# Later places for V and for keys by tokens in a delta-rule kernel's order of transfers

## The chip, the core and the metric

The kernel runs on one core of one Trainium2 chip. The metric is the time of one execution on the device in microseconds; five executions of the kernel before gave a median of 535.37 us (534.04 to 536.3).

Engines are named as in the profile: PE is the matrix engine and PEld its weight loads, DVE the vector engine, ACT the scalar engine, POOL the general engine, SP the engine whose queue issues most of the loads. Each engine runs its own queue strictly in order; between queues there are semaphores.

## The reference

Two blocks follow each other. The first is a delta-rule attention over 768 tokens for 4 batches, 8 heads and a head size of 48, everything in float32:

```
k_n = k / (norm(k) + 1e-6)
for t in range(768):
    y[t]  = q[t] @ state
    v_old = state.T @ k_n[t]
    state = state + beta[t] * outer(k_n[t], v[t] - v_old)
```

The second takes the result as 3072 rows of 384 numbers, sends each row to one of 8 experts by a hash of its token id, and computes `relu(x @ w1[e]) @ w2[e]` (384 to 1024 to 384) with that expert's weights.

## The kernel before, in words

**Chunks and groups.** The 768 tokens are cut into 24 chunks of 32 tokens (`C = 32`, `NU = 24`). Four chunks make a group (`GC = 4`), so there are six groups, numbered from 0. The four batches lie in the four quarters of the 128 partitions. Inside a chunk the recurrence over tokens is replaced by a triangular system, so that the state only has to be carried from chunk to chunk.

**Work for a group.** `load_turn(g, a, b)` (line 359) loads the keys (`a = 0`, tile `Kt`) or queries (`a = 1`, tile `Qt`) of 128 tokens for one batch: eight loads of 192 KB for a group. `turn(g, a, b)` (line 381) transposes such a tile on PE (L389) and copies it on ACT into `KQ` (L394). There is one `Kt` and one `Qt` buffer for each batch, so a group's tile can only be loaded when the same tile of the group before has been transposed. `gram(c)` (line 400) then multiplies keys with keys and queries for a chunk on PE (L415); ACT copies the first product into `GK` (L425), and DVE multiplies the second with a triangular mask into `GQ` (L431). Group 0 has its own form for the keys (L447). `inverse(g)` (line 494) takes the four `GK` of a group, transposes them (`NT`, L506), normalizes, writes the diagonal of U on ACT (L530), and inverts the triangular matrices by 31 elimination steps on DVE, each a multiply (L546) and an add (L544). `turn_back(g)` transposes U into `TU` (L560).

**Work for a chunk.** `spread_t` makes `Tz` from `TU` on ACT (L472), `scale_v(c)` multiplies `V` with the keys' norms on DVE into `V1` (L491; two buffers), and `chunk(c)` (line 594) is the recurrence: PE forms the state's answer to the keys (L581, with V1 added by L613), ACT copies it to R (L618), PE solves (L632), ACT copies W (L646), PE updates the state (L653) with the keys by tokens `K4`, ACT copies the new state (L676), and PE forms the chunk's output (L689), which ACT copies (L698) and POOL scatters into a scratch array in the order of the experts (L703). Chunk 0 has no state yet and solves straight from V1.

**The loads by chunk.** `load_k(c)` (line 365) loads the keys by tokens into one of three `K4` buffers, four loads of 48 KB, one for each batch. `load_v(c)` (line 372) does the same for V with four buffers. All `Kt`, `Qt`, `K4` and `V` loads of the attention block go through SP's queue.

**The order.** No engine's order is written by hand. `task(...)` (line 190) only notes a piece of work: its engine, an estimated duration, what it reads and writes, and some hints. `order()` (line 223) is a list scheduler that runs when the kernel is built. It walks through a model of all engines, and each time takes, on the engine that can start first, the ready task with the longest estimated chain of work behind it (`rest`). A transfer of n KB occupies the model's single transfer channel for `n * 6.3` ns (line 333). The argument `hold` is the earliest time in the model at which a task that waits for nothing else counts as ready (lines 249 and 352). It isn't a wait on the chip: it only moves the task in the order that results. The instructions are then emitted in the order of the planned start times, with the semaphores that the data need. Mask multiplies carry `boost=1e6` and so go ahead of everything else that is ready on DVE. Where the plan leaves PE idle for more than 380 ns, up to a planned time of 80,000 ns, `fill` puts some matmuls into a free bank (L986).

**After the chunks** come the eight experts (lines 1003 to 1163): rows are gathered (L1017), transposed (L1036), multiplied with both weight arrays (L1044, L1078, L1060) and scattered to the output (L1067).

Of the kernel before, what the change touches and what calls it, by code (L numbers as in the profile page):

```python
# [20 lines left out]
def kernel(  # L21
# [88 lines left out]
    with ExitStack() as phase1:  # L110
# [19 lines left out]
        def quarter(b):  # L130
            return slice(C * b, C * b + C)
# [58 lines left out]
        def task(eng, ns, reads, writes, emit, words=0, kb=0, more=0, boost=0, job=None,  # L190
                 hold=0, claim=(), slack=0):
            deps = {writer[r] for r in reads if r in writer}
            for w in writes:
                deps |= readers.get(w, set())
                if w in writer:
                    deps.add(writer[w])
            i = len(tasks)
            deps.discard(i)
            tasks.append(dict(eng=eng, ns=ns, deps=deps, emit=emit, words=words, kb=kb,
                              more=more, boost=boost, job=job, hold=hold,  # L200
                              claim=claim, slack=slack))
            for r in reads:
                readers.setdefault(r, set()).add(i)
            for w in writes:
                writer[w] = i
                readers[w] = set()
            return i
# [157 lines left out]
        def load_k(c):  # L365
            dst = K4s[c % 3].rearrange("p u r d -> p (u r) d")
            for b in range(B):
                task("SP", 500, (), (f"k4{c % 3}{b}",), lambda b=b: nc.sync.dma_start(
                    out=dst[quarter(b), :, 0:D], in_=k_r[b][c * C:(c + 1) * C]), kb=48,
                    hold=16000)  # L370

        def load_v(c):
            for b in range(B):
                task("SP", 500, (), (f"v{c % 4}{b}",), lambda b=b: nc.sync.dma_start(
                    out=Vs[c % 4][quarter(b)], in_=v_r[b][c * C:(c + 1) * C]), kb=48,
                    hold=16000)

        def four(name):
            return tuple(f"{name}{b}" for b in range(B))
# [496 lines left out]
        def note():  # L876
# [29 lines left out]
            for g in range(1, GC):  # L906
                for b in range(B):
                    for a in range(2):
                        load_turn(g, a, b)
                if g == 1:  # L910
                    for c in range(2):
                        load_k(c)
                        load_v(c)
                    load_v(2)
                    load_v(3)
                for b in range(B):
                    for a in range(2):
                        turn(g, a, b)
                if g < GC - 1:
                    for c in range(GC * g, GC * g + GC):  # L920
                        gram(c)
                    inverse(g)
                    if g == 1:
                        turn_back(1)
# [4 lines left out]
            for c in range(NU):  # L929
                g, cc = divmod(c, GC)  # L930
                if c + 2 < NU:
                    load_k(c + 2)
                if c + 4 < NU:
                    load_v(c + 4)
                if c + 1 < NU:
                    spread_t(c + 1)
                    masks_of(c + 1)
                chunk(c)
                if c + 2 < NU:
                    scale_v(c + 2)  # L940
                if cc == GC - 1 and 2 <= g + 2 < NG:
                    turn_back(g + 2)
                if g + 4 < NG and cc == GC - 1:
                    for b in range(B):
                        for a in range(2):
                            load_turn(g + 4, a, b)
                            turn(g + 4, a, b)
                n = c + 3 * GC
                if n < NU:
                    gram(n)  # L950
                if n < NU and n % GC == GC - 1:
                    inverse(n // GC)
# [239 lines left out]
```

## Time and profile before

| what | value |
|---|---|
| median of five executions | 535.37 us |
| the profiled execution's own time | 536.39 us |
| its span on the core | 534.6 us |
| first chunk's solve begins (L632) | 67.62 us |
| last row store issued (L703) | 238.5 us |
| PE busy, share of the span | 481.8 us, 90% |
| DVE busy | 246.4 us, 46% |
| ACT busy | 186.3 us, 35% |
| POOL busy | 96.6 us, 18% |
| mean granted clock of PE | 0.954 |

The profile is of one execution. A line of a timeline gives the start and the duration in us, the engine, the line of the kernel, the operation, what it writes and reads, and in brackets how long the engine stood idle before it and on whose account. In a table by stretches each engine's busy time stands with the number of its instructions in brackets, and the last three columns are the clock granted to PE (1 is full speed), the mean busy share of the transfer engines, and GB/s. In the slices each digit is the busy share of 13.4 us, in tenths.

The SP queue issues, in this order: the keys and queries of group 0 (0.9 to 9.0 us), the keys and queries of group 1 (9.1 to 19.4), 20 loads of V and K4 for the first chunks (19.4 to 33.2), group 2 (33.2 to 43.2), 16 more loads of K4 and V (43.2 to 53.3), group 3 (53.3 to 61.9) and group 4 (61.9 to 71.5). From then on loads of V and K4 alternate as the chunks free their buffers.

The time at which the state-carrying copy W (L646) of a chunk begins shows the pace of the chunks: chunk 0 at 69.3 us, 4 at 99.1, 8 at 129.6, 12 at 160.4, 16 at 190.0, 20 at 221.3.

### The profile page before, as it was taken

What the parts mean: (1) busy time and instruction counts of PE and PEld (TensorE: products, weight loads), DVE (VectorE), ACT (ScalarE), POOL (GpSimd) and SP (SyncE); (2) the same over time, 40 slices, a digit from 0 to 9 for tenths busy, and PEclk for the clock granted to TensorE, in tenths of its full rate; (3) what the DMA queues carried; (4) which work ended last, traced back from release to release, by engine and by line L of the source; (5) the groups of instructions that cost most, each with busy time, mean ns of one, the idle gap of its engine ahead of it and who ended that gap; (6) DMA issues with size and microseconds to landing.
All of it is one profiled execution on the core that took longest, in us unless ns stands there. A gap on an engine that the chain in (4) does not pass through costs nothing. (4 is left out here: it accounts for less than half of the span.)

```text
span 534.6 us, 15771 instructions
## 1 busy us (share of the span) xinstructions
PE 481.8 (90%) x6700; PEld 322.0 (60%) x6700; DVE 246.4 (46%) x775; ACT 186.3 (35%) x406; POOL 96.6 (18%) x139
## 2 busy tenths in 40 slices
PE   8868699899999898865999999999999999999990
PEld 6646577677777677653565555555655556555650
DVE  9688779998999998523120111201202111111100
ACT  4623497988798785320101001101011010100100
POOL 6000011111111112226113111302303111102010
PEclk9968699999999999995999999999999999999996
DMA  9767983574343344713704417107134171340000
GB/s 143 136 108 113 163 143 85 120 156 98 84 86 78 77 99 147 205 48 110 273 14 175 150 34 255 60 13 273 55 119 167 39 258 37 109 155 28 14 28 15
DMA packets 119127, 59.75 MB, mean 112 GB/s; under 512 B 104202, under 2 KB 112614, under 8 KB 119056
## 3 DMA queue, kind: packets, MB, share of 16 engines
q1 hardware_dynamic: 103664, 22.04, 23.1%
q10 hardware_dynamic: 10272, 22.14, 11.6%
q0 software_dynamic: 5120, 14.56, 8.1%
q8 instruction: 53, 0.87, 0.7%
q14 instruction: 18, 0.15, 0.1%
HBM read 49.90 MB, written 10.42 MB: 113 GB/s over the span
## 5 line engine op out<-in xcount | busy, mean ns | idle before, releaser
L1044 PE MATMUL h_ps<-xT,w_sb 128*128 128x378 f32 (+3 forms) x384 | 132.1, 498 | 4.0 <-DVE h_sb L1049 3.3
L1044 PEld LDWEIGHTS h_ps<-xT,w_sb 128*128 128x128 f32 x384 | 72.7, 193 | 56.4 <-issue 17.4
L1049 DVE TENSOR_SCALAR h_sb<-h_ps 128x378 f32<-128x378 f32 (+3 forms) x32 | 18.0, 563 | 152.2 <-PE h_ps L1044 152.2
L1078 PE MATMUL oT_ps<-h_sb,w_sb 128*128 128x424 f32 (+1 forms) x192 | 68.0, 507 | 0.0
L546 DVE TENSOR_TENSOR tmp<-U,Ni 128x60 f32<-128x60 f32 (+15 forms) x186 | 62.0, 338 | 4.5 <-ACT U L530 1.1
L1060 PE MATMUL o_ps<-w_sb,h_sb 128*126 128x384 f32 (+1 forms) x192 | 63.6, 486 | 0.0
L544 DVE TENSOR_TENSOR U<-U,tmp 128x60 f32<-128x60 f32 (+15 forms) x186 | 62.0, 339 | 3.3
L1067 POOL DMA_INDIRECT out_dram<-o_sb,idx_i x28 | 27.7, 988 | 194.7 <-ACT o_sb L1066 144.2
L703 POOL DMA_INDIRECT x_scratch<-x_sb,slot x24 | 24.7, 1030 | 193.8 <-ACT MT L472 69.6
L1078 PEld LDWEIGHTS oT_ps<-h_sb,w_sb 128*128 128x128 f32 x192 | 35.5, 190 | 25.6 <-issue 13.9
L1047 ACT ACTIVATE h_sb<-h_ps 128x378 f32<-128x378 f32 (+3 forms) x32 | 15.9, 496 | 99.2 <-PE h_ps L1044 83.3
L1060 PEld LDWEIGHTS o_ps<-w_sb,h_sb 128*126 128x126 f32 (+1 forms) x192 | 35.0, 186 | 23.7
L676 ACT ACTIVATE S<-psS 48x384 f32<-48x384 f32 (+1 forms) x92 | 42.8, 465 | 13.6 <-PE psS L653 8.7
L1066 ACT COPY o_sb<-o_ps 126x384 f32<-126x384 f32 (+3 forms) x16 | 7.7, 479 | 83.5 <-PE o_ps L1060 69.0
L1017 POOL DMA_INDIRECT xg<-x_scratch,rows_i x28 | 28.3, 1010 | 34.3 <-DVE idx_i L1028 18.1
L653 PE MATMUL psS<-W,K 32*128 32x96 f32 x736 | 26.8, 280 | 5.1 <-ACT W L646 4.9
L1080 ACT COPY oT<-oT_ps 128x424 f32<-128x424 f32 (+1 forms) x8 | 4.0, 499 | 75.3 <-PE oT_ps L1078 75.3
L1038 DVE COPY xT<-xT_ps 128x318 f32<-128x318 f32 (+3 forms) x28 | 14.0, 499 | 33.8 <-PE xT_ps L1036 33.8
L689 PEld LDWEIGHTS psY<-W,MT 64*64 64x64 f32 x704 | 22.7, 134 | 10.0 <-issue 9.1
L653 PEld LDWEIGHTS psS<-W,K 32*128 32x128 f32 x736 | 23.0, 186 | 8.3 <-ACT W L646 6.7
L689 PE MATMUL psY<-W,MT 64*64 64x48 f32 x704 | 25.9, 220 | 0.2 <-issue 0.2
L472 ACT ACTIVATE Tz<-TU,kmask 128x256 f32<-128x256 f32 x40 | 24.9, 727 | 1.0 <-DVE TU L560 0.9
(162 smaller groups left out, 604.0 us busy)
## 6 DMA issues: line engine op xcount, KB each, us to landing
w_sb<-in_moe_w_dram ACTq DMA_DIRECT2D x14, 1536.0 KB
Kt<-in_k_dram SPq DMA_DIRECT2D x24, 192.0 KB
Qt<-in_q_dram SPq DMA_DIRECT2D x24, 192.0 KB
V<-in_v_dram SPq DMA_DIRECT2D x96, 48.0 KB
K<-in_k_dram SPq DMA_DIRECT2D x96, 48.0 KB
w_sb<-in_moe_w_dram SPq DMA_DIRECT2D x3, 512.0 KB
w_sb<-in_moe_w_dram SPq DMA_DIRECT2D x4, 384.0 KB
xg<-x_scratch,rows_i POOLq DMA_INDIRECT x28, 3.1
```

The source lines that it names most:

```text
L472: lambda e=e: nc.scalar.activation(out[:, :, e].rearrange(order_of), in_.rearrange(order_of), ACT.Copy, scale=kmask[:, e:e + 1]))
L544: nc.vector.tensor_tensor(U[:, n:, 0:n], U[:, n:, 0:n], t, op=ALU.add)
L546: nc.vector.tensor_tensor(t, U[:, j:n, 0:n].to_broadcast([P, m, n]), Ni[:, j, n:, None].to_broadcast([P, m, n]), op=ALU.mult)
L653: nc.tensor.matmul(psS[:, b, 2 * D * u:2 * D * u + 2 * D], lhsT=K4[quarter(b), u].rearrange("p r d -> p (r d)"), rhs=W[quarter(b), 2 * u:2 ...
L676: nc.scalar.activation(put, get, ACT.Copy)
L689: nc.tensor.matmul(py[rows, h], lhsT=MT[rows, h].rearrange("p e i -> p (e i)"), rhs=W[rows, h], start=(c == 0 and h == 0), stop=True, skip ...
L703: put = nc.gpsimd.indirect_dma_start(out=x_dram[:, :], out_offset=bass.IndirectOffsetOnAxis(ap=slot[:, c:c + 1], axis=0), in_=x_sb, in_off ...
L1017: nc.gpsimd.indirect_dma_start(out=xg, out_offset=None, in_=x_dram[:, :], in_offset=bass.IndirectOffsetOnAxis(ap=rows_i[:, c:c + 1], axis= ...
L1044: nc.tensor.matmul(h_ps[:, :width], lhsT=w1_sb[:, co, fo * P:(fo + 1) * P], rhs=xT[:, co, :width], start=(co == 0), stop=(co == CO - 1))
L1060: nc.tensor.matmul(o_ps[0:rows], lhsT=h_sb[:, fo, col * rows:(col + 1) * rows], rhs=w2_sb[:, fo, :], start=(fo == 0), stop=(fo == FO - 1))
L1067: scat = nc.gpsimd.indirect_dma_start(out=out[:, :], out_offset=bass.IndirectOffsetOnAxis(ap=idx, axis=0), in_=o_sb, in_offset=None, bound ...
L1078: nc.tensor.matmul(oT_ps[:, 0:width], lhsT=w2_sb[:, fo, i * P:(i + 1) * P], rhs=h_sb[:, fo, 0:width], start=(fo == 0), stop=(fo == FO - 1))
```

## The change

Two arguments `hold` become larger for the first chunks. Keys by tokens (K4) of chunks 0 and 1 are held until 40,000 ns of the planner's time and of chunk 2 until 52,000; V of chunks 0 and 1 until 37,000 and of chunks 2 and 3 until 48,000. All of these were held until 16,000 before, and those of later chunks still are.

```diff
         def load_k(c):
             dst = K4s[c % 3].rearrange("p u r d -> p (u r) d")
             for b in range(B):
                 task("SP", 500, (), (f"k4{c % 3}{b}",), lambda b=b: nc.sync.dma_start(
                     out=dst[quarter(b), :, 0:D], in_=k_r[b][c * C:(c + 1) * C]), kb=48,
-                    hold=16000)
+                    hold=40000 if c < 2 else 52000 if c < 3 else 16000)
 
         def load_v(c):
             for b in range(B):
                 task("SP", 500, (), (f"v{c % 4}{b}",), lambda b=b: nc.sync.dma_start(
                     out=Vs[c % 4][quarter(b)], in_=v_r[b][c * C:(c + 1) * C]), kb=48,
-                    hold=16000)
+                    hold=37000 if c < 2 else 48000 if c < 4 else 16000)
```

No load, no computation and no buffer is added or taken away. Since the planner decides the order of everything at once, the order on the other engines may come out different too.

## The prediction

> **What bounds the kernel now.** I read the 40 slices first, then the busy times by stretch, then the waits up to 66 us, then the timelines of DVE, ACT, PE and SP around the longest. The chain that ended last says nothing: it holds only the final scatter. The slices show three stages. Until about slice 4 (67 us) no engine is full; until slice 17 (238 us) PE shows 9 in nearly every slice while 24 chunks follow each other; after that the experts run on a full PE. The change touches loads of the first stage, so the question is what ends that stage late.
>
> ```profile
> PE   8868699899999898865999999999999999999990
> DVE  9688779998999998523120111201202111111100
> ```
> The gate of the first chunk is the inverse of group 0: 31 pairs of DVE steps (L546, L544), begun at 23.22 us, whose last is followed by the transpose into TU; then ACT makes Tz and PE solves chunk 0 (L632, 67.62). DVE runs its queue in order, and three stops stand inside this inverse:
> ```profile
> 39.32 0.29 DVE L431 TENSOR_TENSOR GQ<-psS,mask 128x128 f32<-128x128 f32 x1 [1.33 <-ACT GK L425]
> ...
> 54.58 0.29 DVE L431 TENSOR_TENSOR GQ<-psS,mask 128x128 f32<-128x128 f32 x1 [2.45 <-PE psX L415]
> ...
> 59.85 0.19 DVE L546 TENSOR_TENSOR tmp<-U,Ni 128x31 f32<-128x31 f32 x1 [1.10 <-ACT U L530]
> ...
> 62.05 1.24 DVE L560 STREAM_TRANSPOSE TU<-U 128x1024 f32<-128x1024 f32 x1
> ```
> The bracket is the idle time before the line and who ended it. The next stop is on ACT, after TU is ready at 63.29: Tz stands behind copies of group 3's keys and queries.
> ```profile
> 59.07 0.60 ACT L394 ACTIVATE KQ<-z 128x512 f32<-128x512 f32 x1 [1.96 <-PE z L389]
> 59.56 0.25 ACT L530 ACTIVATE U<-d 128x32 f32<-128x32 f32 x1
> ...
> 65.86 0.60 ACT L394 ACTIVATE KQ<-z 128x512 f32<-128x512 f32 x1 [1.02 <-PE z L389]
> 66.35 2.23 ACT L472 ACTIVATE Tz<-TU,kmask 128x256 f32<-128x256 f32 x4
> ```
> All four lead to one place, the arrival of keys and queries. PE waits for them twice, and SP's queue says why:
> ```profile
> 37.75 0.48 PE L389 MATMUL psS<-ident,Kt 128*128 128x128 f32 x1 [0.70 <-DMA Kt<-in_k_dram]
> 57.95 2.27 PE L389 MATMUL z<-ident,Kt 128*128 128x128 f32 x8 [3.47 <-DMA Kt<-in_k_dram]
> ```
> ```profile
> 15.31 4.07 SPq L363 DMA_DIRECT2D Qt<-in_q_dram  x4
> 19.43 3.71 SPq L374 DMA_DIRECT2D V<-in_v_dram  x4
> ...
> 31.17 1.94 SPq L374 DMA_DIRECT2D V<-in_v_dram  x4
> 33.21 4.10 SPq L363 DMA_DIRECT2D Kt<-in_k_dram  x4
> 37.40 5.77 SPq L363 DMA_DIRECT2D Qt<-in_q_dram  x4
> ...
> 45.80 7.37 SPq L374 DMA_DIRECT2D V<-in_v_dram  x12
> 53.27 3.95 SPq L363 DMA_DIRECT2D Kt<-in_k_dram  x4
> ```
> Between group 1's queries and group 2's keys stand 20 loads of 48 KB (V of chunks 0 to 2, K4 of 0 and 1), 33.2 - 19.4 = 13.8 us, 0.69 us each; group 2's own eight take 10.0 us (1.25 each). Sixteen more small loads (43.2 to 53.3) stand before group 3.
>
> **The change, part by part.** No instruction is added or removed; the hold numbers only let the planner place the small loads later, and its list order then changes on every engine. A hold is no wait on the chip: it orders SP's queue and, through the planned arrival, the users' queues.
>
> 1. Group 2's loads. A load may be sent when its buffer was transposed. PE transposed group 1's keys at 16.89 to 21.28 and its queries at 22.42 to 28.73, so group 2's keys can follow at 19.4 and the last query tile at 28.7 (now 40.9). That one landed 5.6 us after its issue; taken again, group 2 is complete at 34.3, not 46.5. Its transposes and grams (48.4 to 54.4 now) can follow those of group 1, whose PE part ends at 37.0. The stops of 1.33 (PE's gram for it was held up in the run-up to 37.75) and 2.45 lose their cause: **3.78 us**. Bounds: 0 (the stop is PE's own, below) to 3.78.
>
> 2. Group 3's loads follow group 2's transposes, some ten us earlier at the least, in place of 53.3 to 61.9. ACT's copies then no longer stand in front of U's diagonal (1.10) and Tz (66.35 - 63.29 = 3.06): **4.16 us**; bounds 0 and 4.16.
>
> 3. The moved loads: 16 of V, 12 of K4, 28 x 0.69 = 19.3 us of SP. They go out from about 38 to 58, with group 4's eight (10 us) perhaps among them. Needed: V of chunk 0 by its multiply (L491), which must precede the solve at about 60 after the gain; K4 of chunk 0 by its update some 2.2 us later (69.85 against 67.62). Twelve to sixteen small loads are 8.3 to 11 us, so K4 lands by 38 + 11 + 2 = 51 (small loads landed 2 us after issue in most cases): cost **0**, and the cover is some 11 us. V of chunks 2 and 3 is wanted only after chunk 0's solve, where DVE already stood for the same multiply:
> ```profile
> 68.81 0.56 DVE L491 TENSOR_TENSOR V<-V,ntok 128x384 f32<-128x384 f32 x1 [2.58 <-PE psX L632]
> ```
> If V2 is later than that solve, DVE's inverse 1 waits behind the multiply; 0 to 2 us, and chunk 4 is the first that could feel it. I take 0.
>
> 4. With group 3 there early, the grams of chunks 12 and 13 have their buffers free and can slip in before chunk 0: four multiplies of 0.22 us pace on DVE inside the inverse, **+0.88**. What they relieve later (grams between chunks) I count as nothing; up to -2 for the range, as chunks with a gram in them cost 6.9 us and the undisturbed ones from 184 us on 6.4.
>
> 5. PE's clock. It was granted 0.53 in 58 to 66 and 1.00 from 66 on, because group 3's transposes and filler matmuls kept PE busy just before chunk 0:
> ```profile
> 58.00:66.00 8.00, 7.80 (x30) 6.06 (x31) 6.78 (x30) 3.27 (x7) 0.00 (x0) 0.53 1.02 169
> 66.00:69.50 3.50, 2.87 (x46) 2.37 (x44) 0.92 (x3) 3.50 (x7) 0.00 (x0) 1.00 1.11 163
> ```
> (The clock is the third number from the end.) With these gone early PE has little to do for some ten us, and chunk 0 may begin at half clock. Four transposes took 1.06 us at the low clock and 0.66 at the high one, 1.6 times. If the first 4 us of chunk work run so, of which some 2.5 are PE time on the path, that is 2.5 x 0.6 = **+1.5**; bounds 0 (fillers hold it) and +4 (ten us, as long as the low stretch 55.4 to 65.6 of this trace). [...]
>
> 6. PE's own stop. In group 2's grams PE stood from 50.7 to 53.3 with no releaser but "issue" (2.4 us in the waits), while one of the instruction queue's packets (53 packets, 0.87 MB on the page, 16 KB each) came at 50.3 to 51.8. It can return wherever grams run densely; then DVE's 2.45 stays. [...] I take it that DVE is elsewhere in its queue, as PE is now ahead of it; the difference goes to the range.
>
> Sum at chunk 0: -3.78 - 4.16 + 0.88 + 1.5 = **-5.6 us**. It carries to the end if nothing else gates later chunks. TU of group 1 is ready at 93.7 and chunk 4's R at 95.1, so inverse 1 has about 1.4 us to spare; but the same stops held it up, and the 2.58 shifts with chunk 0. Later TU tiles come 8 us or more before need (119.7 against W of chunk 8 at 129.6). The expert stage starts on the last row store and shifts along. The profiled execution took 536.39 (span 534.6), 1.0 above the median 535.37. 536.39 - 5.6 = 530.8, which against the median is **529.8 us**.
>
> **Rivals.**
> *The stops move but stay.* The planner lets DVE's queue meet another PE stop (fetch of code, PE waiting 3.43 us for a mask multiply at 33 to 36.6), so part 1 gives nothing, and the clock and grams eat part of the rest: -4.16 + 0.88 + 1.5 = -1.8, or -0.3 with the clock at 3: some 533.6 to 535. For it: those two stops are no data arrival. Against: the lateness of group 2's data is 12 us, far more than either.
>
> *V and K4 become the gate* (slower). If group 3's last load still goes out at 61.9, because its buffers are freed late by PE's order, the twelve small loads for V of 0 and 1 and K4 of 0 end 8.3 us later and land 2 us after that: chunk 0's update at 72.2, against 69.85 now: +2.3, **537.7**. The point from which it decides: the first V must be issued by about 59.5 for no loss against before, and by 51 for the whole gain. Against: PE's transposes of group 2 are possible from 24 on. For: V and K4 are now ordered behind them in one queue that cannot overtake.
>
> *It does not do what it says*: buffers keep group 2 back anyway. Part 1 denies it: only 28.7 of 40.9 is forced. I give it no share of its own.
>
> **Chances and range.** Forecast 0.62 (all of it faster, 524 to 533). Stops stay 0.17 (0.06 faster, 0.09 same, 0.02 slower). V and K4 late, or another loss of the reshuffled order, 0.21 (0.03 same, 0.18 slower). A measurement here tells 0.3%, 1.6 us, from no change. So faster 0.68, same 0.12, slower 0.20. The forecast's own bounds: -7.94 + 0.88 - 2 = -9.1 (526.3) without a clock loss, +0 where clock takes 4 and part 1 fails. For 8 in 10 I go from 525 to 537: the whole forecast, the stops that stay, and the near end of the late V.
>
> **What would show it.** SP: eight loads of group 2 straight after 19.4, group 3 before the V loads. DVE: no stop over 1 us at a mask multiply between 23 us and TU. TU near 58 instead of 62.05, Tz within half a us of it, solve of chunk 0 near 61 instead of 67.62. The clock after the solve shows part 5. Wrong if L491 waits for V, if SP's first V is past 51, or if the spacing of chunks 0 to 8 grows by what chunk 0 won.

## The result and the profile after

The changed kernel takes **533.44 us** (median of 52 runs, 530.31 to 537.99) against 534.99 of before (94 runs in the same job): ratio 0.9969, 95% interval 0.996 to 0.9979, a gain of 1.6 us. The forecast was a gain of 5.6. The profiled executions took 536.39 and 535.18, 1.4 and 1.7 above these medians.

| in the profiled execution, us | before | after | gain |
|---|---|---|---|
| TU of group 0 begun (L560) | 62.05 | 61.37 | 0.7 |
| Tz begun (L472) | 66.35 | 62.64 | 3.7 |
| first solve (L632) | 67.62 | 64.01 | 3.6 |
| W of chunk 4 | 99.1 | 93.6 | 5.5 |
| W of chunk 8 | 129.6 | 123.5 | 6.1 |
| W of chunk 12 | 160.4 | 155.3 | 5.1 |
| W of chunk 16 | 190.0 | 187.4 | 2.6 |
| W of chunk 20 | 214.2 | 211.6 | 2.6 |
| last row store issued (L703) | 238.5 | 236.3 | 2.2 |
| span | 534.6 | 533.6 | 1.0 |

(Chunk 20 stands at 221.3 in the list ahead of the prediction; the trace has 214.21.)

So two things went otherwise than forecast: 3.6 us were won at the first solve in place of 5.6, and what was won rose to 6 by chunk 8 and then melted. The slices show only that nothing large has moved:

```profile
PE   8865999999998898856999999999999999999990
DVE  7796899998989886512120111201301111111100
```

The SP queue did what the diff says. These are its lines in the timeline (start, duration of the issues, queue, line, what is loaded, how many):

```profile
19.47 4.79 SPq L363 DMA_DIRECT2D Kt<-in_k_dram  x4
24.35 5.08 SPq L363 DMA_DIRECT2D Qt<-in_q_dram  x4
29.53 10.56 SPq L363 DMA_DIRECT2D Kt<-in_k_dram  x4
40.18 3.70 SPq L363 DMA_DIRECT2D Qt<-in_q_dram  x4
43.93 4.53 SPq L374 DMA_DIRECT2D V<-in_v_dram  x6
48.51 1.93 SPq L368 DMA_DIRECT2D K<-in_k_dram  x4
```

Group 2's keys leave at 19.47 in place of 33.21, group 3's at 29.53 in place of 53.27, and the first V at 43.93. The timeline of DVE, ACT and PE around the first solve shows what became of it:

```profile
37.81 0.29 DVE L431 TENSOR_TENSOR GQ<-psS,mask 128x128 f32<-128x128 f32 x1 [0.54 <-ACT GK L425]
...
50.27 0.29 DVE L431 TENSOR_TENSOR GQ<-psS,mask 128x128 f32<-128x128 f32 x1 [3.25 <-PE psS L415]
...
57.43 0.38 DVE L546 TENSOR_TENSOR tmp<-U,Ni 128x31 f32<-128x31 f32 x2 [0.42 <-ACT U L530]
...
60.94 0.51 DVE L431 TENSOR_TENSOR GQ<-z,mask 128x128 f32<-128x128 f32 x2 [1.06 <-ACT GK L425]
61.37 1.24 DVE L560 STREAM_TRANSPOSE TU<-U 128x1024 f32<-128x1024 f32 x1
...
62.64 2.27 ACT L472 ACTIVATE Tz<-TU,kmask 128x256 f32<-128x256 f32 x4
...
63.31 0.55 DVE L491 TENSOR_TENSOR V<-V,ntok 128x384 f32<-128x384 f32 x1
...
64.01 1.14 PE L632 MATMUL psX<-V,Tz 64*64 64x48 f32 x32 [0.31 <-ACT Tz L472]
```

The end of the preparation is as hoped: TU is ready at 62.61 and Tz starts at 62.64; there is no copy in between, and the multiply of V (63.31) waits for nothing. But DVE stands again at a mask multiply, 3.25 us, where 1.33 and 2.45 were to go, and a new stop of 1.06 stands just ahead of TU, at the mask multiply of chunk 12, whose gram now comes before chunk 0. DVE's idle time between 23.2 and 62 us is 7.47, and was 7.50. So the 0.7 by which TU is earlier is no wait that went: the elimination begins 0.35 us earlier (22.87 against 23.22), and two multiplies of V (L491, 1.10 us together) that stood ahead of TU now stand behind it, against two more mask multiplies and some 0.2 us of small work in front. At the stop of 3.25 DVE waits for a gram of PE, and the waits of PE between 26 and 66 us (who waited for whom, total, times, longest) say what PE itself stood for. Before:

```profile
PE psY L415 <- issue: 2.4, 1, 2.4
```

After:

```profile
PE psS L415 <- issue: 5.6, 2, 4.0
```

"Issue" is time without a releaser. PE stands from 45.7 to 49.7 near the end of group 2's grams; a 16 KB packet of the instruction queue comes at 46.63 and PE goes on 3.0 us after that. Before, the packet came at 50.26 and PE went on at 53.24, 3.0 us later.

The clock did not suffer; this is the table by stretches, the clock third from the end:

```profile
48.20:58.50 10.30, 6.58 (x54) 5.20 (x54) 6.85 (x33) 5.35 (x15) 0.00 (x0) 0.51 0.64 117
58.50:62.00 3.50, 3.33 (x129) 2.22 (x131) 2.44 (x13) 1.74 (x4) 0.00 (x0) 0.99 1.05 185
62.00:66.00 4.00, 3.58 (x63) 2.19 (x56) 3.87 (x13) 3.73 (x7) 0.00 (x0) 1.00 0.47 82
```

The later loss shows in the same view, taken from W of chunks 0, 4, 8 and 12 to that of the chunk four on (after the bounds: length, then busy time and instructions of PE, PEld, DVE, ACT, POOL). Before:

```profile
69.30:99.10 29.80, 27.76 (x911) 21.83 (x909) 28.02 (x93) 25.04 (x59) 5.34 (x8) 1.00 0.54 104
99.10:129.60 30.50, 29.39 (x817) 23.22 (x825) 28.10 (x100) 27.12 (x60) 5.20 (x9) 1.00 0.68 143
129.60:160.40 30.80, 30.08 (x814) 23.27 (x812) 29.66 (x100) 26.72 (x59) 4.98 (x8) 1.00 0.37 80
160.40:190.00 29.60, 27.40 (x901) 21.38 (x898) 27.06 (x81) 23.65 (x55) 4.97 (x8) 1.00 0.35 76
```

After:

```profile
65.70:93.60 27.90, 26.39 (x752) 20.75 (x753) 26.51 (x88) 23.34 (x54) 5.40 (x8) 1.00 0.64 132
93.60:123.50 29.90, 28.20 (x840) 21.91 (x835) 28.29 (x103) 25.48 (x58) 3.95 (x6) 1.00 0.63 123
123.50:155.30 31.80, 30.58 (x836) 23.53 (x834) 29.99 (x99) 27.64 (x61) 6.10 (x10) 1.00 0.41 91
155.30:187.40 32.10, 28.54 (x904) 22.37 (x904) 28.38 (x90) 24.09 (x56) 5.13 (x8) 0.95 0.35 75
```

The first eight chunks are 2.5 us quicker, the second eight 3.5 slower. PE has 3294 matmuls between chunks 0 and 16 where it had 3427, since more grams lie ahead of chunk 0 now, and yet the sixteen chunks take 121.7 us, not 120.7. More PE work is not the reason. The last stretch also shows a granted clock of 0.95: 3.4 us at half clock (0.51 granted), from 181.4 on.

### The profile page after: what moved, and what is told of

Read it like the earlier page. It is cut to its first block, busy times and chain, and to the rows that moved or that the text cites. A ratio compares the mean times of both kernels' runs of the same rounds, so it can differ in the third digit from the quotient of the medians.

```text
span 533.6 us, 15751 instructions
## 1 busy us (share of the span) xinstructions
PE 479.0 (90%) x6688; PEld 319.7 (60%) x6688; DVE 241.2 (45%) x775; ACT 186.0 (35%) x406; POOL 96.0 (18%) x139
## 3 DMA queue, kind: packets, MB, share of 16 engines
q1 hardware_dynamic: 103664, 22.04, 23.2%
## 5 line engine op out<-in xcount | busy, mean ns | idle before, releaser
L544 DVE TENSOR_TENSOR U<-U,tmp 128x112 f32<-128x112 f32 (+15 forms) x186 | 61.6, 338 | 3.0
L546 DVE TENSOR_TENSOR tmp<-U,Ni 128x112 f32<-128x112 f32 (+15 forms) x186 | 61.4, 337 | 3.1 <-ACT U L530 0.4
L703 POOL DMA_INDIRECT x_scratch<-x_sb,slot x24 | 25.1, 1046 | 194.3 <-ACT MT L472 123.7
L1078 PEld LDWEIGHTS oT_ps<-h_sb,w_sb 128*128 128x128 f32 x192 | 35.5, 190 | 25.6 <-issue 13.9
L632 PE MATMUL psX<-R,Tz 64*64 64x48 f32 x672 | 24.2, 220 | 1.6 <-ACT R L618 1.0
```

What stands on the lines that cost most here:

```text
L544: nc.vector.tensor_tensor(U[:, n:, 0:n], U[:, n:, 0:n], t, op=ALU.add)
L546: nc.vector.tensor_tensor(t, U[:, j:n, 0:n].to_broadcast([P, m, n]), Ni[:, j, n:, None].to_broadcast([P, m, n]), op=ALU.mult)
L632: nc.tensor.matmul(pws[i][rows, h], lhsT=Tz[rows, h].rearrange("p e i -> p (e i)"), rhs=R[rows, h], start=(h == (hs.start if split else 0) ...
L703: put = nc.gpsimd.indirect_dma_start(out=x_dram[:, :], out_offset=bass.IndirectOffsetOnAxis(ap=slot[:, c:c + 1], axis=0), in_=x_sb, in_off ...
L1078: nc.tensor.matmul(oT_ps[:, 0:width], lhsT=w2_sb[:, fo, i * P:(i + 1) * P], rhs=h_sb[:, fo, 0:width], start=(fo == 0), stop=(fo == FO - 1))
```

## The experiments

Every run is set against runs of the kernel before in its own job (a series of runs on one chip), for the jobs differ: a chunk that nothing disturbs takes 6.4 us in the first and the fourth of the five jobs and 6.9 us in the others (its solve 1.65 in place of 1.13), and before has medians of 534.99, 542.7, 543.0, 535.9 and 543.0. A measured time is the median in us, and in brackets stand its ratio to before and the 95% interval of that. The theory at first: the start was won in part, and later chunks gave some of it back. The rivals: a gain at chunk 0 isn't worth its length, for later chunks wait for something that doesn't move; DVE is full and sets the pace; the new order of the work is worse.

**The pair again, three times.** The kernel before and the changed one, unchanged, in the same job with the others.

> The kernel before, unaltered, for a second profile of it beside the next three. Both theories: first solve near 67 us. For the split of the time into three stretches (to the first solve, from there to the last row store, from there to the end): the third stretch was 295.7 to 297.3 us in the six profiles so far and followed the end of the half-clock stretch at the experts' start; with that end 14 to 15 us after the last store it should be 295.7 to 296.3 here, with 16 to 17 us 297.

> The changed kernel, unaltered, timed beside the kernel before on this chip, with a second profile. Theory (the lead is won before the first solve and not much of it is lost for good): first solve 3 to 4 us before that of the kernel before, last row store 2 to 3.5 us before, time 1 to 3 us less. Rival (the later chunks give it back): last store less than 1 us ahead.

> The changed kernel unchanged, as the partner of the three others. On the first chip it stood 1.5 us below before, on the second 2.2; 1.5 to 2.3 us below before is expected by all theories. In its profile: lead over before 3.6 us at the first solve, 5 to 6 at chunk 8, 2.5 to 3.2 at chunk 16.

> The changed kernel unchanged, the partner of the two others: 1.5 to 2.3 us below before by both theories; a half-clock window between 165 and 190 in its profile by the theory, as in the three taken so far.

Measured: before 542.47 in a single, profiled execution; after 540.49 (0.996, interval 0.9938 to 0.9981), 533.91 (0.9949, 0.9918 to 0.998) and 540.84 (0.9953, 0.9922 to 0.9983). In the first of these pairs the first solve came at 65.19 (near 67 had been expected) and 61.70, 3.5 earlier; the leads at chunks 4, 8, 12 and 16 were 4.7, 6.1, 4.1 and 3.2, and 2.4 at the last store. The picture of the first profiles repeats. The second time the changed kernel has no profile of before beside it; against the first profile of before, chunk 8 leads by 5.8 and chunk 16, behind 6.8 us at half clock, by 0.6, where 2.5 to 3.2 had been expected. What varies too is the stop at the mask multiply: 3.25 us in the first profile of the changed kernel, 1.23 in the second, with the same order. And the kernel before varies at the start: with the queues in its order TU0, the TU of group 0, begins at 59.4 to 62.5 us in four profiles, and DVE stands 4.8 to 7.7 us inside that inverse; in the changed order TU0 begins at 59.1 to 61.6 in eleven, and DVE stands 4.9 to 7.7. Where a job has profiles of both orders, the first solve is 1.5 to 3.6 us earlier in the changed one; what is steady is that Tz no longer waits (0.0 us after TU, against 2.2 to 3.1). The half-clock stretch between 165 and 190 us appears in three profiles of the changed kernel (181.4, 168.1 and 181.4) and not in the fourth, so the last expectation failed on that point.

**Does a shift of chunk 0 carry?** ACT makes the first copy of chunk 0's Tz seven times, in the changed kernel and in that of before. Order and work are otherwise the same.

```diff
-                         lambda e=e: nc.scalar.activation(
+                         lambda e=e: [nc.scalar.activation(
                              out[:, :, e].rearrange(order_of), in_.rearrange(order_of),
-                             ACT.Copy, scale=kmask[:, e:e + 1]))
+                             ACT.Copy, scale=kmask[:, e:e + 1])
+                             for _ in range(times if e == 0 else 1)][-1])
...
-                   c >= LATE, "p h i -> p i h")
+                   c >= LATE, "p h i -> p i h", times=1 if c else 7)
```

> The changed kernel, but the first ACT copy that makes chunk 0's Tz (L472) is done seven times in place of once, which holds the first solve back by 6 x 0.56 = 3.4 us (0.56 from 2.23 us for four). Nothing else changes, the order least of all. It takes most of the 3.6 us away that the change won at chunk 0. Carry theory (each microsecond at chunk 0 goes through to the end, and what is missing at the end was lost later by the order): 3.0 to 3.8 us slower than the changed kernel in the same job, so about 1 us slower than before. Absorb theory (the chunks between 8 and 16 wait for other work that does not move with chunk 0): 0 to 1.5 us slower than the changed kernel, so the start is worth little.

> The same 3.4 us of repeated copies put into the kernel before. Carry theory: 3.0 to 3.8 us slower than before. Absorb theory: 0 to 1.5 us.

Measured: 539.36 (1.0073, 1.0045 to 1.01), 5.4 above the changed kernel's 533.91; and 543.59 (1.0141, 1.0096 to 1.0187), 7.7 above before. More than both theories said, and the profile shows where: with the hole on PE the granted clock falls to 0.50. This is the table by stretches of the changed kernel with the copies:

```profile
66.00:79.70 13.70, 12.03 (x144) 8.49 (x148) 7.78 (x19) 8.47 (x17) 1.17 (x1) 0.50 0.42 76
79.70:90.00 10.30, 9.12 (x260) 7.39 (x252) 6.75 (x17) 6.47 (x14) 1.74 (x4) 1.00 0.63 130
```

From 55.8 to 66.0 the clock was 1.00. PE stood 4.9 us for Tz, until 67.67; the half clock begins inside this hole, and chunk 0 and its successor run in its 13.7 us. What matters is how the lag goes on, read from the W copies against the same kernel without the copies:

```
lag, us          c0   c1   c4   c8   c12  c16  last store  span
changed kernel   4.1  9.1  9.1  8.9  8.9  6.0  6.5         6.7
kernel before    5.2  6.0  6.0  5.8  6.0  5.9  6.1         6.7
```

The row of before is against its first profile, whose undisturbed chunks are as long. From chunk 1 to chunk 12 the lag passes on within 0.3 us in both orders. The upper row falls at chunk 16 because its partner's profile has 6.8 us of half clock at 181.4; against the first profile of the changed kernel, with 3.4 us of it there, the lag is 9.0 at chunk 12, 8.0 at chunk 16 and 8.6 at the last store. So the rival that later chunks wait for something fixed is out: **with the order given, a delay of the start goes through one for one from chunk 1 on.** (An earlier start with the order kept was not run.) What was lost after chunk 8 is then put down to the new order, with the clock that comes with it.

**The stop of PE.** To see whether it belongs to a piece of work or to a place in the instruction stream, 256 and 128 PE instructions are left out ahead of it: parts of the grams of group 0.

```diff
-                task("PE", 200, held, names, lambda u=u: go(u), words=32, job=(job, 0))
+                task("PE", 200, held, names,
+                     lambda u=u: go(u) if g or u < 2 else None, words=32, job=(job, 0))
```

> The changed kernel with half of the matmuls left out of the four grams of group 0 that make only masks (u of 2 and 3): 128 matmuls and their weight loads, 256 instructions of PE's queue at 17 to 26 us, the size of one instruction packet of 16 KB. Order kept, no load moved. Theory (PE's stop of 4.0 us at 45.7, which the profile puts down to issue, is a wait for instructions): the stop moves 256 instructions further, behind the grams of group 2, DVE's stop of 3.25 us at 50.27 falls under 1 us, and TU of group 0 is ready at 58 to 59.5 instead of 62.6; if DVE is the rail, most of these 3 us last to the end (530 to 531.5). Rival (PE waits there for data or for a bank): the stop stays at the same matmuls and TU is earlier by less than 1 us.

> The changed kernel with a quarter of the matmuls left out of the four mask-only grams of group 0 (u of 3): 64 matmuls and their weight loads, 128 instructions, half of an instruction packet. In the run that left out 256, a whole packet, the packets' borders fall on the same later instructions as before, and PE's stop stayed where it was; half a packet moves the borders by 128 instructions. Theory (the stop of 4.0 us is a wait for the next packet): it leaves the place 24 matmuls before the end of group 2's grams, DVE's stop of 2.1 to 3.3 us at the mask multiply falls under 1 us, TU of group 0 starts 2 to 3.5 us earlier than in the unaltered run beside it. Rival (data or bank): same place, same stop, TU less than 1 us earlier. If the chunks then hold what is won before the first solve, the time is 2 to 3.5 us under the changed kernel; if the chunks are bound by something of their own that does not start earlier, under 1 us.

The second has `u < 3`. Measured: 539.81 (0.9957, 0.994 to 0.9973) and 542.40 (0.9993, 0.9964 to 1.0021). (The profile with 256 left out is of an execution of 553.0 us; 30.7 us at half clock in it lie between 120 and 151 us, far behind this place.) The waits of PE between 26 and 66 us, with 256 left out:

```profile
PE psS L415 <- issue: 5.8, 2, 3.6
```

With 128 left out:

```profile
PE psS L415 <- issue: 5.1, 2, 2.7
```

The counts of PE's instructions (weight loads and matmuls, as far as the trace has them) show where the long stop lies. It comes after 2222 instructions in all four profiles with the order of before and after 2221 in all eleven with the changed order. That alone says little, for nearly the same matmul stands there (the 735th and the 740th of the 768 gram matmuls, L415, of groups 0 to 2). It comes after 1965 in both kernels with less code, 256 fewer. With 256 left out that is the same matmuls as before, as the rival of data or a bank said: the stop did not move behind group 2's grams, and TU0 came at 61.42 (61.37 in the changed kernel's first profile), so that expectation failed. But a border at every 256 instructions would put one on the same matmuls too. Only the run with 128 tells the two apart: there the stop moved to other matmuls, 128 instructions earlier in the work. A shorter stop ahead of it agrees: it comes after 1456 instructions in the changed kernel, after 1200 with 256 left out, and after 1456 again with 128 left out. So the stop keeps to a count and not to a piece of work, in steps of some 256 (1200, 1456, 1965 and 2221). That fits the packets of the instruction queue: the page has 53 of 16 KB, and 13,400 matmuls and weight loads for the kernel before, by which I estimate some 253 for each packet. With 128 left out DVE's stop was 1.56 us, against 1.23 in the changed kernel beside it, and TU0 came later (60.9 against 59.1), so the expectation of a gain failed as well. No kernel without the stop was run, and what the 3 us would be worth was not shown.

**Is DVE the rail**, the engine that sets the pace? Four of the 31 elimination steps are left out for groups 2 to 5, 14.6 us of DVE, in both kernels.

```diff
             def step(j, last):
+                if g >= 2 and 14 <= j < 18:
+                    return
```

> The changed kernel with four of the 31 elimination steps (14 to 17) left out of the inverses of groups 2 to 5; the planner still counts them, so every queue keeps its order. DVE loses 4 x 2 x 0.457 = 3.7 us in each of four inverses, 14.6 us in all, from about 82 us on. Theory (DVE is the rail): in the changed kernel the chunks were 5.5 to 6.1 us ahead at chunks 4 and 8 and fell back to 2.6 at chunk 16 because DVE's queue, which is never idle for long from 70 us on, cannot run earlier; with DVE lighter the lead stays, and this kernel ends 4 to 6 us before the same cut of the kernel before (run beside it). Rival (the new order of the later chunks costs it): every queue has the same order as in the changed kernel, so the lead shrinks as it did and the two cut kernels differ by 1 to 2.5 us.

> The kernel before with the same four steps left out of the inverses of groups 2 to 5, order of the queues kept. Theory (DVE is the rail): 2 to 5 us faster than the kernel before, and 4 to 6 us slower than the cut changed kernel. Rival (order): whatever it gains, the cut changed kernel is only 1 to 2.5 us ahead of it.

Measured: the changed kernel 539.63 (0.9946, 0.9927 to 0.9965), the kernel before 542.30 (1.0001, 0.998 to 1.0023). In before, 14.6 us less of DVE give nothing: chunks 8 and 16 at 129.4 and 191.6, against 130.0 and 192.5 with all the steps (the profile of before in the next job, whose chunks are as long). DVE, busy 27 to 30 of some 30 us in every stretch of four chunks, is **not** what sets the pace there. The two lightened kernels differ by 2.7 us, just past what the rival allows (1 to 2.5) and well short of the theory's 4 to 6. In the changed kernel the ratio is a little under that of the full one (0.9949 to 0.9969), which did not run in this job, with intervals that overlap; so for the changed order a small share of DVE is not ruled out.

**Where does the order lose?** The order of the changed kernel up to the planned solve of chunk 12, or 8, and the order of before from there. The core of it:

```diff
+            seq_1, start_1 = plan(late)
+            first = [i for i in seq_1 if start_1[i] < start_1[marks[12]]]
+            seq_2, start_2 = plan(early)
+            both = first + [i for i in seq_2 if i not in set(first)]
```

> Nothing left out. Up to the planned solve of chunk 12 every queue has the order of the changed kernel; all that is left then follows in the order of the kernel before. Chunk 12 was 5.1 us ahead in the changed kernel, chunk 16 2.6. Rival (order): the later order is that of before, so the lead of about 5 us lasts to the last row store and the time is 3.5 to 5 us under the kernel before. Theory (DVE is the rail): the inverses of groups 4 and 5 still wait their turn on DVE, the lead is 2 to 3 us at chunk 16 and the time 1 to 2.5 us under the kernel before.

> The changed kernel's order up to the planned solve of chunk 12, the order of before from there, once more with more rounds, next to the changed kernel on one chip. If the changed order loses its lead after chunk 12 by its own (waits of chunks 12 to 16 and the holes in PE's work that halve the clock there): 0.8 to 1.5 us faster than the changed kernel, about 0.994 of before. If it was only the noise of one job: equal to the changed kernel within 0.5 us.

> The changed kernel's order up to chunk 12, that of before from there, beside the two others on one chip. Theory: as h1, 0.8 to 1.5 us below the changed kernel. Rival, nothing but noise: within 0.5 us of it.

> Nothing left out. Order of the changed kernel up to the planned solve of chunk 8, then that of the kernel before. In the first profile chunk 8 was 6.1 us ahead and chunk 16 2.6. Theory (the order of chunks 8 to 16 gives back 3.5 us): lead of 5 to 6 us at chunk 16, time 4 to 5 us under the kernel before. Rival (the same work is only spread otherwise over the chunks, so that a lead at chunk 8 is one of the moment): lead of 1.5 to 3 us at chunk 16 and time 1 to 3 us under the kernel before, like the changed kernel beside it.

Measured, cut at 12: 539.40 (0.9946, 0.9927 to 0.9966), 532.75 (0.9947, 0.9927 to 0.9967) and 539.74 (0.9923, 0.9895 to 0.9951). The first, 3.3 us under before, lies between its theory (1 to 2.5) and its rival (3.5 to 5). Twice the changed kernel ran beside it, and had a median 1.2 and 1.1 us higher, as expected; the intervals overlap. It is the best version that I have, by medians 3.2 to 3.3 us below before, and clearly below it. Why it is better than the changed kernel is only half clear. In one job its profile goes from chunk 12 to 16 in 30.2 us, and the changed kernel's, with 6.8 us of half clock, in 34.0; in the other the two take 31.4 and 31.6 and both issue the last store at 243. And part of the loss lies ahead of the cut: from chunk 8 to 12 the changed order takes 1.0 us more than before in the first pair of profiles and 2.0 in the second. Of its 33 runs 3 have a mean granted clock under 0.96, of the 36 of the changed kernel beside the other experiments 10. Among runs with a clock of 0.963 or more the means are 1.8, 2.4 and 2.4 below before for the changed kernel in its three later jobs, and 2.4, 2.4 and 2.8 for this one in its three. So a good part of the difference seems to be the clock.

Cut at 8 the lead did not last: 543.30 (0.9994, 0.9969 to 1.0019), and chunk 16 came 2.2 us later than in before; neither expectation held. Chunks 8 and 9 cost 10.8 us each, at half clock from 127.6 to 137.8, and 7 of 12 runs have a clock of 0.952 or less, against 4 of 29 of before. The seam itself makes a hole (PE busy 1.31 of the 3.41 us from 123.97 on); the run says nothing clean on the order.

**Group 5's early start.** In the changed order DVE begins the inverse of group 5 between the last steps of group 4's. DVE's timeline of the changed kernel:

```profile
169.63 1.24 DVE L506 STREAM_TRANSPOSE NT<-GK 128x1024 f32<-128x1024 f32 x1
173.81 0.68 DVE L535 SCALAR_TENSOR_TENSOR Ni<-NT,d 128x496 f32<-128x496 f32 x1
177.31 1.24 DVE L560 STREAM_TRANSPOSE TU<-U 128x1024 f32<-128x1024 f32 x1
```

Before, this NT came at 177.4, behind TU (175.8). ACT, in order too, then waits 1.3 us for the norms of group 5 (171.21) with W of chunk 14 behind it (172.5), and 0.6 us for TU with a Tz of chunk 16 (178.59) and W of chunk 15 behind that (179.6). The planner was told to begin group 5 only after TU.

```diff
+            i, j = marks
+            after[j].append(i)
-            wait = [len(t["deps"]) for t in tasks]
+            wait = [len(t["deps"]) + (x == i) for x, t in enumerate(tasks)]
```

(`i` is the NT of group 5, `j` the TU of group 4.)

> The changed kernel, but the planner may begin the inverse of group 5 (L506 and the normalization behind it) only when group 4's TU has been made (L560). Its order is the changed kernel's up to chunk 12. In the three profiles of the changed kernel DVE makes group 5's NT (1.24 us) at 169.6 to 172.4 and its norms and Ni among the last steps of group 4's inverse, and TU of group 4 comes at 177.3 to 180.1; in the kernel before (175.8) and with the order of before from chunk 12 (172.3, 175.0) NT comes after TU. Theory, DVE's early start of group 5 costs the lead: TU of group 4 at 172.5 to 174.5, W of chunk 14 at 170.5 to 171.8 (now 172.5 and 173.0), chunk 12 to 16 in 30 to 31.5 us (now 32.1, 31.9, 34.1), no half-clock window between 165 and 190, and the median 0.8 to 2 us below the changed kernel's. Rival, the lead is lost to other holes of that order or to PE's work: TU earlier, but chunk 12 to 16 still over 31.8 us and the median within 0.5 us of the changed kernel.

Measured: 542.35 (0.9982, 0.9954 to 1.0011), 1.5 above the changed kernel; the rival had said within 0.5. DVE's timeline shows that the order came as wanted:

```profile
180.72 1.25 DVE L564 STREAM_TRANSPOSE TU<-U 128x1024 f32<-128x1024 f32 x1
181.89 1.20 DVE L510 STREAM_TRANSPOSE NT<-GK 128x1024 f32<-128x1024 f32 x1
```

From chunk 12 to 16 it takes 32.5 us, the changed kernel beside it 31.6: **this theory falls.** From the end of the solve to W it now takes 0.60 us in four chunks, against 2.06, but the state copies now came later after the update (3.17 against 1.46). Part of the 1.5 us is something else: half clock from 95.8 to 106.1, where chunk 5 cost 3.6 more than the partner's. A wait taken out of this order came back at the next link.

## Why the prediction was right and wrong

**Direction and transfers: right.** The hold numbers moved group 2 to 19.47 and group 3 to 29.53 as worked out, and V and K4 cost nothing: first V at 43.93, with 51 as the bound. The rival *V and K4 become the gate* is out.

**Part 2: its larger term came in full**, the copies ahead of Tz (3.06 to 0.03); that is the bulk of the 3.6 us at the first solve. The stop before U's diagonal shrank from 1.10 to 0.42, but DVE's idle time as a whole did not, so by itself it did not bring TU forward.

**Part 1 is the step that failed.** It counted 3.78 us for DVE's stops; DVE's idle time stayed (7.50, 7.47), and TU, forecast near 58, began at 61.37. The stop of 1.33 did go (that multiply waits 0.54 now), but the 2.45 came back as 3.25. The prediction had the cause in its hands, part 6: a PE stop of 2.4 us without releaser at an instruction packet. It then decided that DVE would be "elsewhere in its queue". The runs show that the stop sits at a fixed number of instructions, 2221 or 2222 with none left out, and that group 2's grams still run across this border after the change; so DVE, which goes through its queue in order (in the changed kernel an add of the elimination, whose multiply ended at 47.0, came behind the mask multiply of 50.27, at 53.10), meets it again. In the first pair part 1's lower bound, 0, was the right value; in the second DVE's idle time in the inverse fell by 1.0 us (5.88 to 4.87), and over all profiles the two orders cover the same range. What TU would gain without the stop was not shown. Most of the 53 packets bring no such stop: the first two profiles have only one and two stops of PE over 1 us without a releaser in the whole run. At the border that falls among group 2's grams, PE stood 1.9 to 4.0 us in all seventeen profiles.

**Part 4** put +0.88 for four mask multiplies inside the inverse. Two of them, 0.5 us, stood there, the other two behind TU (62.70). But the gram of chunk 12 also brought the stop of 1.06 us just ahead of TU, a wait that the prediction put at nothing. Neither did it count what V's later place gave TU, 1.10 us. **Part 5** was mis-sized: +1.5 forecast, 0 measured. The low clock ended at 58.6, and with fillers and transposes PE was busy 3.33 of 3.50 and 3.58 of 4.00 us up to 66, at 0.99 and 1.00. The fear was well founded in kind: with the repeated copies and a hole of 4.9 us there the clock was 0.50 for 13.7 us, and another 5.0 us were lost (lag 4.1 at chunk 0, 9.1 at chunk 1).

**"It carries to the end if nothing else gates later chunks."** In its literal sense shown for a delay: with a given order it goes through one for one from chunk 1 on. But the change also gives a new order to all engines, and that one wins 2.5 us up to chunk 8 and loses 3.5 until chunk 16. The prediction named the lead's rise (grams in front, up to -2) and gave "another loss of the reshuffled order" a chance, but its sum has no term for one. That this loss is the order's is what the shift runs leave; which of its waits makes it stays open. DVE's load (tried in the kernel before), more PE work (counted) and group 5's early start (moved) are not it; cutting back to the old order at chunk 12 helped by about 1.1 us by medians, in part by the clock.

**From 2.2 to 1.6.** The last store came 2.2 us earlier, the span ended 1.0 earlier. In both profiles the first experts run at half clock (0.50 granted) from 239.5 or 239.7 to 253 us, and the earlier start only put more of their work into it: PE was busy 8.60 us of this stretch, 6.60 before. In other runs it ends elsewhere; the medians, over many runs, show 1.6 to 2.5.

In time the rival *the stops move but stay* (533.6 to 535) was nearest. The stop did stay, and chunk 12's gram ate its share; but the clock's part did not come, and the time is so near because 1.4 of the 3.6 us won at the first solve were gone at the last store, for which that rival had no term. That it comes so near is luck.

## What to carry to other kernels

Ask of every stop that is to vanish which of its causes moves with the edit: the one here sat at a count of instructions (2222 before, 2221 after) and stayed there, and DVE met it again (2.45 us, then 3.25). When a planner makes the order, a changed hint buys two things, the thing meant and a new order for everything behind it; a forecast needs a term, and a range, for the second. A delay of the start goes through at its length here (6.0 us at chunk 1 and 6.1 at the last store, in the kernel before), apart from what a halved clock adds (5.0 us in the changed kernel), so to see whether a lost lead is due to a fixed wait or to the order, delay the start alone and follow the lag.

## What the runs showed of the hardware

The half-clock stretches (0.50 granted) that the profiles show were 3.4, 6.8, 10.2, 13.7 and 17.1 us long, one to five times 3.41, and 30.7, nine times that, in the execution of 553.0 us. Their length doesn't follow the hole that went before: in the runs with the repeated copies a PE stop of 4.9 us was followed by 13.7 us at half clock in the changed kernel, one of 5.2 us by only 3.4 in the kernel before. Nor do these profiles show one amount of busy time of PE below which half clock came. In the fourth job's profile of the changed kernel PE was busy 2.03 of 3.41 us, then came half clock:

```profile
177.99:181.40 3.41, 2.03 (x72) 1.76 (x63) 3.31 (x9) 2.83 (x7) 1.19 (x2) 0.99 0.30 84
181.40:188.20 6.80, 6.80 (x116) 5.28 (x110) 5.14 (x13) 4.10 (x9) 1.19 (x2) 0.50 0.41 74
```

In the third job 2.70 of 3.41 us busy came ahead of a half-clock window:

```profile
164.69:168.10 3.41, 2.70 (x111) 2.16 (x107) 2.20 (x8) 2.14 (x6) 0.42 (x2) 1.00 0.19 64
168.10:171.51 3.41, 3.41 (x90) 2.17 (x90) 3.21 (x10) 2.03 (x5) 0.00 (x0) 0.50 0.27 54
```

In the first profile of before 2.19 of 3.41 did not bring one:

```profile
178.24:181.65 3.41, 2.19 (x72) 1.66 (x64) 3.04 (x12) 3.29 (x9) 0.00 (x0) 1.00 0.57 134
181.65:185.06 3.41, 2.94 (x95) 2.53 (x96) 2.99 (x12) 3.00 (x8) 1.18 (x2) 1.00 0.33 91
```

At the start of the experts 13.7 or 17.1 us at half clock (0.50) came in every profile. Over the seventeen profiles the time from the last store to the end rises from 295.7 to 297.4 us as this stretch ends 13.9 to 17.1 us after the last store, some 0.46 us for each microsecond.
